# Q and K of two batches transposed by 32x32 blocks on VectorE, from blocks that DMAs set out beforehand

## The chip, the cores and the metric

The kernel runs on one core of a Trainium2 chip. A core has TensorE (matrix products and transposes into PSUM), VectorE, ScalarE, GpSimd (POOL) and SyncE (SP), each with its own queue of instructions in a fixed order, and 16 DMA engines. The metric is the device time of one execution in microseconds, the median of the runs shown. The profile is of one execution; times within it are counted from the start of its span.

## The reference

Two stages on float32 data. First a linear attention with decay, for 4 batches, 8 heads, 768 positions and a head dimension of 64; then a Fourier mixing of its output along sequence and model dimension, a normalization, and an MLP (512 to 2048 to 512) with a residual.

```
for b in range(nb):                                  # blocks of positions
    intra = einsum('bhic,bhjc->bhij', qb, kb) * Dmask
    intra = einsum('bhij,bhjd->bhid', intra, vb)
    inter = einsum('bhid,bhde->bhie', qb * lam_pow, kv_state)
    out[block] = intra + inter
    kv_state = lam_block * kv_state + einsum('bhsd,bhse->bhde', kb * rev_pow, vb)

x = out as (batch, 768, 512)
u = x + real(fft(fft(x, axis=1), axis=2))
un = (u - mean(u)) / sqrt(var(u) + 1e-6)
result = u + relu(un @ w_ch1) @ w_ch2
```

The two MLP weights come as 8-byte floating point numbers, so they are loaded as pairs of 32-bit words and decoded on the core.

## The kernel before

Attention is computed in chunks of 128 positions, six to a batch, all eight heads together. A chunk (`attn_chunk`, L257) loads k, q and v with one DMA each: rows of 64 numbers (256 B) go to `[128 positions, 8 heads, 64]`. The product of q and k contracts over the head dimension, so both must stand with the head dimension on the partitions. For this TensorE transposes pairs of heads, four 128x128 transposes for k (L272) and four for q (L277), into PSUM, and ScalarE copies the results to `kT` and `qT` (L274, L279). From these come the scores (L290, two halves of the array, one head in each), which VectorE multiplies by the decay (L294). The natural k is also multiplied by its decay on GpSimd (L268, `kd`) for the state (L305); this isn't done in the last chunk of a batch. From the second chunk on, VectorE makes `qs` from the transposed q in PSUM (L282) for the product with the state (L318). L322 multiplies scores and v, and L329 turns the output back.

The Fourier stage of a batch (`fft_ln`, L427) needs rows in mirrored order, which GpSimd gathers from a copy of x in device memory (`mirror_a`, `mirror_b`). `fold_a` and `fold_b` add and subtract rows and columns on VectorE into two pairs of tiles, `fe` and `fo`, the first with 128 rows and the second with 65 (L365 to L416). Products with tables follow on TensorE (L440, then L453 to L458), then the normalization. `mirror_a` gathers the rows that `fold_a` needs into tiles of their own, `r0` and `r1`, from the pool `fp`, which has one buffer for each name.

The weights are loaded in 32 pieces of 512 KB (`load_weights`, L219). Each goes into a `raw` buffer of the pool `hp_`, which has five buffers of this shape, and is decoded by VectorE and ScalarE together (L232 to L240). The MLP of a pair of tiles (`mlp`, L549) takes four buffers of the same pool for its hidden values (`hr`), so that the last weight loads and the first MLP group share five buffers. Four of the twelve groups go through `mlp` (L555, L569), mixed with the front stages of the batches 1 to 3; the other eight are done after them by `late` (L623), with a scheme of seven products for eight (L637, L684).

The order of work: every engine executes its instructions in program order, and that order is set before the run. The kernel is written as generators which yield an estimate of the TensorE time of each piece; `weave` (L723) interleaves two of them in a given ratio of these estimates, and at L770 and L771 the ratio for the rest of the front stages against the MLP groups is worked out from `t_rest`. A planner then orders the instructions of each engine by dependencies and its own estimates, sets the waits, and assigns buffers. So an instruction that stands early in an engine's order and has to wait holds up everything behind it on this engine, but nothing on the others that doesn't depend on it. All loads, and the stores of `ud`, `utd` and the output, are issued by SP in one order; ScalarE issues the stores of x for the gathers. In the program each DMA that SP issues also waits until the one about eight places before it in the queue has landed.

Names used below: `ld` is the pool of k, q and v (two buffers for each name), `at` the pool of the attention's intermediate tiles, `dram` a pool of tiles in device memory, `ALU.mult` elementwise multiplication.

Of the kernel before, what the change touches and what calls it, by code (L numbers as in the profile page):

```python
# [10 lines left out]
F32 = mybir.dt.float32  # L11
U32 = mybir.dt.uint32
# [63 lines left out]
def kernel(  # L76
# [10 lines left out]
    nc = tc.nc  # L87
    B, H, S, D = q.shape
    DM = H * D
    DFF = moe_w_ch1.shape[1]  # L90
    C = 128
    NC = S // C
    HC = NC // 2
    HP = H // 2
# [26 lines left out]
    ld = front_pool("ld", 2)  # L121
# [16 lines left out]
    def new(pool, shape, tag, **kw):  # L138
        cnt[0] += 1
        return pool.tile(shape, F32, tag=tag, name=f"{tag}{cnt[0]}", **kw)  # L140

    def psum_a(shape):
        return new(pa, shape, "pa")
# [58 lines left out]
    def row_of(j, n=128):  # L202
        return bass.IndirectOffsetOnAxis(ap=ix[0:n, j:j + 1], axis=0)
# [4 lines left out]
    w1v = moe_w_ch1.rearrange("(c p) f -> p c f", p=128)  # L208
    w2v = moe_w_ch2.rearrange("(c p) m -> p c m", p=128)
    WP = 512  # L210

    def load_tables(i):
        if i == 1:
# [5 lines left out]
    def load_weights(dst, src):  # L219

        if src.dtype == F32:
            nc.sync.dma_start(dst, src)
            return
        raw = hp_.tile([128, 2 * WP], U32, tag="hr", name=f"raw{cnt[0]}")
        pw = ep.tile([128, WP], U16, tag="pw", name=f"pw{cnt[0]}")
        cnt[0] += 1
        nc.sync.dma_start(raw, src.bitcast(U32))
        lo, hi = raw[:, 0:2 * WP:2], raw[:, 1:2 * WP:2]
        top = raw.bitcast(U16)[:, 3:4 * WP:4]
        lof, d = lo.bitcast(F32), dst.bitcast(U32)  # L230

        nc.vector.tensor_scalar(pw, top, 0x7FF0, None, op0=ALU.bitwise_and)  # L232
        nc.scalar.activation(pw, pw, AF.Relu, bias=cvt[:, 0:1], scale=-1.0)
        nc.scalar.activation(pw, pw, AF.Relu, bias=cvt[:, 1:2], scale=-8.0)
        nc.vector.scalar_tensor_tensor(pw, top, 0x8000, pw, op0=ALU.bitwise_and, op1=ALU.bitwise_or)  # L235

        nc.vector.tensor_scalar(d, hi, 0x000FFFFF, None, op0=ALU.bitwise_and)
        nc.scalar.activation(lof, lo, AF.Copy, scale=2.0 ** -52)
        nc.vector.scalar_tensor_tensor(dst, d, 2.0 ** -20, lof, op0=ALU.mult, op1=ALU.add)
        nc.vector.scalar_tensor_tensor(dst, dst, 1.0, pw.bitcast(BF16), op0=ALU.add, op1=ALU.mult)  # L240
# [8 lines left out]
            yield 1.0  # L249


    xs, xn_, xd = {}, {}, {}

    def pair(t, hp):
        return t[:, 2 * hp:2 * hp + 2, :].rearrange("p a d -> p (a d)")

    def attn_chunk(b, c):  # L257
        rows = slice(c * C, (c + 1) * C)
        kt, qt, vt = (new(ld, [C, H, D], nm) for nm in ("k", "q", "v"))
        for t, src in ((kt, k), (qt, q), (vt, v)):  # L260
            nc.sync.dma_start(t, src[b, :, rows, :].rearrange("h p d -> p h d"))
        if b == 0:
            load_tables(c)

        last = c == NC - 1
        if not last:
            kd = new(at, [C, H, D], "kd")
            nc.gpsimd.tensor_tensor(kd, kt, kpow, op=ALU.mult)  # L268

        ptk = psum_a([128, HP, C])  # L270
        for hp in range(HP):
            nc.tensor.transpose(ptk[:, hp, :], pair(kt, hp), ident)  # L272
        kT = new(at, [128, HP, C], "kT", bufs=2)
        nc.scalar.copy(kT, ptk)  # L274
        ptq = psum_a([128, HP, C])
        for hp in range(HP):
            nc.tensor.transpose(ptq[:, hp, :], pair(qt, hp), ident)  # L277
        qT = new(at, [128, HP, C], "qT", bufs=2)
        nc.scalar.copy(qT, ptq)  # L279
        if c > 0:  # L280
            qs = new(at, [128, HP, C], "qs")
            nc.vector.tensor_tensor(qs, ptq, qpow, op=ALU.mult)  # L282
        yield 1.2


        mm = nc.tensor.matmul
# [68 lines left out]
        nc.gpsimd.memset(t, 0.0)  # L355

    gather = nc.gpsimd.indirect_dma_start
    eo, r1s = {}, {}

    def fold_x(b, a, n, i, lo, hi):  # L360

        e, o = eo[b][a]
        tt = nc.vector.tensor_tensor

        tc.keep_in_program_order(tt(e[0:n, i, 0:DM], lo, hi, op=ALU.add))  # L365
        tc.keep_in_program_order(tt(o[0:n, i, 0:DM], lo, hi, op=ALU.subtract))
        tt(e[0:n, i, 1:HM], e[0:n, i, 1:HM], e[0:n, i, HM:DM - 1], op=ALU.add)
        tt(o[0:n, i, 1:HM], o[0:n, i, 1:HM], o[0:n, i, HM:DM - 1], op=ALU.subtract)

    def mirror_a(b):  # L370

        xa = xd[b][0]
        r1 = r1s[b] = [new(fp, [128, DM], f"r{a}") for a in range(2)]

        eo[b] = [(new(fp, [128, 2, 2 * W], f"fe{a}"), new(fp, [128, 2, 2 * W], f"fo{a}")) for a in range(2)]
        for a, n in enumerate(BLK):
            gather(out=r1[a][0:n], out_offset=None, in_=xa[:, :], in_offset=row_of(a, n))
        for t in range(2, HC):
            u = xs[b, HC + t] = new(xp, [128, DM], "x")
            gather(out=u[:, :], out_offset=None, in_=xa[:, :], in_offset=row_of(2 + t))  # L380
# [6 lines left out]
            xs[b, t] = xn_.pop((b, t))  # L387

    def fold_a(b):
        r1 = r1s.pop(b)  # L390
        for a, n in enumerate(BLK):
            fold_x(b, a, n, 1, r1[a][0:n], xn_[b, HC + a][0:n])

    def fold_b(b):

# [371 lines left out]

    run(weave(part(fr, 2 * t_chunk), weave(part(back, FO * 1.7 - 1.0), w, 0.9), 1.5))
    run(w)
    t_rest = 3 * t_front - 6 * t_chunk  # L770
    run(weave(fr, back, (len(PLAIN) * t_mlp - FO * 1.7 - 25.0) / t_rest))  # L771
    front_end.close()
    s2.wp = ctx.enter_context(tc.tile_pool(name="ws", bufs=1, side="left", reuse_waits="tile"))
# [43 lines left out]
```

## Time and profile before

| what | value |
|---|---|
| median of three runs | 882.87 us (881.8 to 887.67) |
| the profiled execution | 881.96 us, span 879.7 us |
| mean granted TensorE clock | 0.982 of full speed |
| TensorE matmul busy | 805.3 us, 92% |
| TensorE weight loads busy | 640.9 us, 73% |
| VectorE busy | 443.9 us, 50% |
| ScalarE busy | 199.1 us, 23% |
| GpSimd busy | 91.0 us, 10% |
| DMA queue of SP | 122816 packets, 57.51 MB, 25.4% of 16 engines |

The page lists each engine's busy time over the span. A TensorE matmul's end is modelled and overlaps with the next, so the distance between starts tells what one costs in a full stretch. The page divides the span into 40 slices of 22 us, with a digit of busy tenths for each engine. Groups of instructions are shown as line, engine, operation, output and inputs, shapes and count, then busy time and mean duration, then the idle time before them and what ended it. The chain of waits is followed back from the last instruction: at every step to what released it. SPq is SP's queue of DMA issues, with the time the issue itself took.

By its place in the profile, the execution has three stretches: to about 186 us the weights are loaded and decoded while batches 0 and 1 go through the attention; to about 443 us the Fourier stage of batch 1, the batches 2 and 3 and the first four MLP groups; from there to the end the eight other groups.

### The profile page before, as it was taken

What the parts mean: (1) busy time and instruction counts of PE and PEld (TensorE: products, weight loads), DVE (VectorE), ACT (ScalarE), POOL (GpSimd) and SP (SyncE); (2) the same over time, 40 slices, a digit from 0 to 9 for tenths busy, and PEclk for the clock granted to TensorE, in tenths of its full rate; (3) what the DMA queues carried; (4) which work ended last, traced back from release to release, by engine and by line L of the source; (5) the groups of instructions that cost most, each with busy time, mean ns of one, the idle gap of its engine ahead of it and who ended that gap; (6) DMA issues with size and microseconds to landing.
All of it is one profiled execution on the core that took longest, in us unless ns stands there. A gap on an engine that the chain in (4) does not pass through costs nothing.

```text
span 879.7 us, 11692 instructions
## 1 busy us (share of the span) xinstructions
PE 805.3 (92%) x4596; PEld 640.9 (73%) x4596; DVE 443.9 (50%) x1022; ACT 199.1 (23%) x451; POOL 91.0 (10%) x108
## 2 busy tenths in 40 slices
PE   4775768689999999999999999999999999999997
PEld 3564556454877557864884888888888888888886
DVE  4678969862562347425597454125611563045410
ACT  3654426630223102211210220012100220012100
POOL 2214411201021202102000000000000000000000
PEclk9989889899999999999999999999999999999999
DMA  9898426710065604643154001110111000110010
GB/s 230 228 234 253 109 84 154 229 67 26 23 142 131 166 25 115 127 87 99 37 152 105 19 1 49 48 48 1 49 48 36 13 1 9 40 48 1 1 37 24
DMA packets 128830, 72.43 MB, mean 82 GB/s; under 512 B 111200, under 2 KB 112744, under 8 KB 128776
## 3 DMA queue, kind: packets, MB, share of 16 engines
q1 hardware_dynamic: 122816, 57.51, 25.4%
q0 software_dynamic: 2496, 7.87, 2.7%
q10 hardware_dynamic: 3464, 6.30, 2.0%
q8 instruction: 36, 0.59, 0.3%
q14 instruction: 18, 0.15, 0.0%
HBM read 50.68 MB, written 20.99 MB: 81 GB/s over the span
## 4 chain that ended last, share of the span: by engine, by line
PE 71%; DVE 8%; issue 6%; DMA 4%; POOL 1%; ACT 1%; POOLq 0%; DVEq 0%; ACTq 0%
PE p L637 22%; PE p L684 22%; PE pm L555 8%; PE pm L569 8%; PE pa L440 3%; DMA raw<-in_moe_w_ch_dram 3%; PE pa L322 2%; PE pa L290 1%; DMA x<-xb,ix 1%; PE pa L318 1%; DVE pw L235 1%; PE pa L305 1%; PE pa L329 1%; PE pa L272 1%; PE pa L277 1%
## 5 line engine op out<-in xcount | busy, mean ns | idle before, releaser
L555 PE MATMUL pm<-ut,w 128*128 128x256 f32 x512 | 123.1, 389 | 10.9 <-ACT hr L563 9.2
L555 PEld LDWEIGHTS pm<-ut,w 128*128 128x128 f32 x512 | 95.0, 193 | 28.0 <-ACT hr L563 10.2
L569 PE MATMUL pm<-w,hr 128*128 128x512 f32 x256 | 114.9, 597 | 0.0
L637 PE MATMUL p<-ur,w 128*128 128x256 f32 x384 | 93.6, 380 | 0.1
L569 PEld LDWEIGHTS pm<-w,hr 128*128 128x128 f32 x256 | 47.1, 190 | 51.7 <-issue 51.1
L637 PEld LDWEIGHTS p<-ur,w 128*128 128x128 f32 x384 | 73.0, 190 | 10.6 <-issue 0.5
L637 PE MATMUL p<-us,w1s 128*128 128x256 f32 x256 | 65.2, 379 | 0.0
L684 PE MATMUL p<-w,hs 128*128 128x256 f32 x256 | 58.0, 380 | 0.5 <-DVE y L705 0.5
L684 PE MATMUL p<-w,ha 128*128 128x256 f32 x256 | 57.9, 379 | 0.0
L684 PE MATMUL p<-w2s,hs 128*128 128x256 f32 x256 | 57.9, 379 | 0.0
L545 POOL DMA_INDIRECT out_dram<-y,ix x12 | 11.8, 982 | 428.9 <-DVE y L708 368.4
L684 PEld LDWEIGHTS p<-w,hs 128*128 128x128 f32 x256 | 48.6, 190 | 7.4 <-DVE y L705 0.9
L684 PEld LDWEIGHTS p<-w,ha 128*128 128x128 f32 x256 | 48.7, 190 | 6.5
L637 PEld LDWEIGHTS p<-us,w1s 128*128 128x128 f32 x256 | 48.7, 190 | 6.5
L684 PEld LDWEIGHTS p<-w2s,hs 128*128 128x128 f32 x256 | 48.7, 190 | 6.5
L664 ACT COPY ha<-p 128x256 f32<-128x256 f32 x32 | 11.9, 372 | 172.8 <-PE p L637 172.8
L322 PE MATMUL pa<-sc,v 128*64 128x128 f32 x384 | 33.1, 298 | 11.3 <-DVE sc L294 11.3
L282 DVE TENSOR_TENSOR qs<-pa,qpow 128x512 f32<-128x512 f32 x20 | 13.8, 689 | 51.6 <-ACT qT L279 51.5
L322 PEld LDWEIGHTS pa<-sc,v 128*64 128x64 f32 x384 | 24.5, 147 | 19.4 <-DVE sc L294 14.6
L290 PE MATMUL pa<-qT,kT 64*128 64x128 f32 x384 | 29.4, 291 | 9.8 <-ACT qT L279 9.8
L290 PEld LDWEIGHTS pa<-qT,kT 64*128 64x128 f32 x384 | 24.5, 193 | 18.9 <-ACT qT L279 15.5
L675 DVE TENSOR_TENSOR ha<-p,ha 128x256 f32<-128x256 f32 x32 | 13.6, 425 | 45.6 <-ACT ha L674 45.5
(142 smaller groups left out, 1188.1 us busy)
## 6 DMA issues: line engine op xcount, KB each, us to landing
raw<-in_moe_w_ch_dram SPq DMA_DIRECT2D x32, 512.0 KB, 5.0
k<-in_k_dram SPq DMA_DIRECT2D x24, 256.0 KB, 4.4
q<-in_q_dram SPq DMA_DIRECT2D x24, 256.0 KB, 4.0
v<-in_v_dram SPq DMA_DIRECT2D x24, 256.0 KB, 3.9
ud<-x SPq DMA_DIRECT2D x16, 256.0 KB, 2.0
utd<-uq SPq DMA_DIRECT2D x64, 64.0 KB, 2.2
u<-ud SPq DMA_DIRECT2D x16, 256.0 KB, 2.6
ur<-utd SPq DMA_DIRECT2D x8, 512.0 KB, 4.4
```

The costliest lines, as they stand in the source:

```text
L235: nc.vector.scalar_tensor_tensor(pw, top, 0x8000, pw, op0=ALU.bitwise_and, op1=ALU.bitwise_or)
L282: nc.vector.tensor_tensor(qs, ptq, qpow, op=ALU.mult)
L290: mm(pss[hi][:, hp, :], lhsT=kT[HD[hi], hp, :], rhs=qT[HD[hi], hp, :], start=True, stop=True)
L322: mm(po[HD[hi], hp, :], lhsT=vt[:, 2 * hp + hi, :], rhs=sc[hi][:, hp, :], start=(c == 0 and hp == 0), stop=(hp == HP - 1), skip_group_chec ...
L440: mm = nc.tensor.matmul(ps[0:m, n, :], lhsT=piece(a, i, n), rhs=cs[0:rows, a, i in (2, 3), n, :], start=(a == 0), stop=(a == 1))
L545: nc.gpsimd.indirect_dma_start(out=out.rearrange("b s d -> (b s) d"), out_offset=row_of(2 + HC * (b + 1) + T - HC), in_=y[:, :], in_offset ...
L555: nc.tensor.matmul(ps, lhsT=w1[:, c, 128 * fc:128 * fc + 128], rhs=ut[:, c, :], start=(c == 0), stop=(c == KO - 1))
L569: nc.tensor.matmul(ps, lhsT=hr[fc // 4][:, fc % 4, 128 * i:128 * i + 128], rhs=w2[:, fc, :], start=(fc == 0), stop=(fc == FO - 1))
L637: nc.tensor.matmul(ps, lhsT=s2.A[a][:, kt, 128 * i:128 * i + 128], rhs=U[b][:, kt, :], start=(first and kt == 0), stop=(kt == 1), skip_gro ...
L664: nc.scalar.copy(a11, two(X))
L675: V.tensor_tensor(a22, two(Z), a22, op=ADD)
L684: nc.tensor.matmul(ps, lhsT=h[a][:, s, i, :], rhs=s2.B[b][:, i, :], start=(first and i == 0), stop=(i == HF - 1), skip_group_check=True)
```

## The change

For batches 2 and 3 (`TURNED`) k and q no longer go through TensorE's transposes and ScalarE's copies. Instead:

- `move_blocks` copies k and q of a batch within device memory into a tile `moved`, 16 DMAs for each of k and q, so 64 in all. One takes, for one half of the head dimension of a head and all 768 positions, pieces of 32 numbers (128 B). Four neighbouring positions stand together behind each other in the new tile. The copies of batch 2 are placed on SP behind the weight load that is ninth from the end, those of batch 3 behind the last one, by an order edge on SP alone. They are traced after the loop over the weights.
- A chunk loads its part of `moved` with one DMA each for k and q, 2 KB for each partition, and one VectorE instruction transposes all 32x32 blocks of it, with an output pattern that puts positions in order again, straight into `kT` and `qT`. So 24 VectorE transposes stand in the place of 96 TensorE transposes and 24 ScalarE copies. `qs` is computed from `qT` in SBUF and no longer from PSUM.
- The natural k is still loaded where `kd` is made (five of six chunks); the natural q isn't in these batches. The new block tile of k (`kb`) takes two buffers in `ld`; q's block tile shares the name and buffers of q.
- `r0` and `r1` are gone: the gather goes into a part of `fo`, and the fold writes its sum to `fe` and then its difference over the gathered rows.
- The first yield of a chunk of these batches is 0.3 and not 1.2, and `t_rest` is smaller by as much.

The diff, at its core:

```diff
+    def move_blocks(b, after):
+        for nm, src in (("k", k), ("q", q)):
+            m = moved[b, nm] = dram.tile([4, NC, 32, HP, 4, 32], F32, name=f"moved_{nm}{b}")
+            for a in range(4):
+                for hp in range(HP):
+                    with tc.issue_after(after):
+                        nc.sync.dma_start(m[a, :, :, hp].rearrange("c n t d -> (c n) t d"),
+                                          src[b, 2 * hp + a // 2, :, 32 * (a % 2):32 * (a % 2) + 32]
+                                          .rearrange("(n t) d -> n t d", t=4))
...
-        nc.sync.dma_start(raw, src.bitcast(U32))
+        loads.append(nc.sync.dma_start(raw, src.bitcast(U32)).ins)
...
+        def turned(nm, load, src):
+            t = new(ld, [128, HP * C], load)
+            nc.sync.dma_start(t, moved[b, src][:, c].rearrange("a n h t d -> a n (h t d)"))
+            tT = new(at, [128, HP, C], nm, bufs=2)
+            nc.vector.transpose(tT.rearrange("p h (n t) -> p h t n", t=4),
+                                t.rearrange("p (h t d) -> p h t d", h=HP, t=4))
+            return tT
+        if blocks:
+            kT, qT = turned("kT", "kb", "k"), turned("qT", "q", "q")
+            ptq = qT
+            if not last:
+                kt = natural("k", k)
+        else:
+            kt, qt = natural("k", k), natural("q", q)
+        vt = natural("v", v)
...
+        if not blocks:
             ptk = psum_a([128, HP, C])
             for hp in range(HP):
                 nc.tensor.transpose(ptk[:, hp, :], pair(kt, hp), ident)
...
-        yield 1.2
+        yield 0.3 if blocks else 1.2
...
-            gather(out=r1[a][0:n], out_offset=None, in_=xa[:, :], in_offset=row_of(a, n))
+            gather(out=eo[b][a][1][0:n, 1, 0:DM], out_offset=None, in_=xa[:, :], in_offset=row_of(a, n))
...
-            fold_x(b, a, n, 1, r1[a][0:n], xn_[b, HC + a][0:n])
+            fold_x(b, a, n, 1, eo[b][a][1][0:n, 1, 0:DM], xn_[b, HC + a][0:n])
...
     run(w)
-    t_rest = 3 * t_front - 6 * t_chunk
+    for b in TURNED:
+        move_blocks(b, loads[-9 + 8 * (b - TURNED[0])])
+    t_rest = 3 * t_front - 6 * t_chunk - 0.9 * NC * len(TURNED)
```

## The prediction

> **What bounds the kernel now.** I read the page's slices first, then the chain of waits, then each engine's timeline where the chain changes hands.
>
> ```profile
> PE   4775768689999999999999999999999999999997
> DVE  4678969862562347425597454125611563045410
> DMA  9898426710065604643154001110111000110010
> ```
>
> A slice is 22 us. From the tenth on (198 us) TensorE is at 9 tenths, so whatever TensorE loses after that point is added to the end, and its work removed there comes off. Before it, TensorE waits for the weights. The DMA row looks free from 176 to 242 us (1, 0, 0). The chain of waits from 160 to 226 us tells how the first stretch ends:
>
> ```profile
> 166.81 4.12 DMA raw<-in_moe_w_ch_dram
> ...
> 173.51 0.68 DVE pw L235
> ...
> 174.22 3.61 DMA raw<-in_moe_w_ch_dram
> ...
> 182.77 0.62 DVE pw L235
> ...
> 183.91 1.99 PE pm L555 x8
> 185.90 13.75 PE pm L569 x32
> ```
>
> A weight load lands, VectorE decodes it, the freed buffer lets the next load go or becomes the `hr` tile of the first MLP group. TensorE's L555 and L569 start when this ends. I call the last nine of the 32 loads A to I (A issued at 150.70, E at 166.81, G at 174.22, H at about 177.05, when F's decode is done, I at about 180.66, when G's is).
>
> VectorE after that (timeline, 208 to 217 us):
>
> ```profile
> 208.58 0.42 DVE L415 TENSOR_TENSOR fo<-fo 128x256 f32<-128x256 f32 x1
> 208.93 0.42 DVE L416 TENSOR_TENSOR fo<-fo 128x256 f32<-128x256 f32 x1
> 217.10 0.42 DVE L575 TENSOR_TENSOR y<-pm,x 128x256 f32<-128x256 f32 x1 [7.76 <-PE pm L569]
> ```
>
> It ends the fold of batch 1's first half, which TensorE needs for L440 at 209.62, and is idle for 7.76 us. The rows to be removed, in the full stretch (TensorE timeline, batch 3):
>
> ```profile
> 358.20 0.60 PE L329 MATMUL pa<-ident,oT 128*128 128x128 f32 x4
> 358.64 0.60 PE L272 MATMUL pa<-ident,k 128*128 128x128 f32 x4
> 359.08 0.60 PE L277 MATMUL pa<-ident,q 128*128 128x128 f32 x4
> 359.51 0.81 PE L555 MATMUL pm<-ut,w 128*128 128x256 f32 x3
> ```
>
> Starts are 0.44 us apart: that, and not the 293 ns mean of one, is what four transposes cost a full TensorE.
>
> **What the Trainium skill says.** (1) "DMA: Bandwidth & Descriptors", Queues, rings and completion order: each DMA engine consumes the descriptors of one queue in ring order. The trace agrees: loads E, G, H and I land at 170.93, 177.83, 180.60 and 184.28, in order of issue. So a copy put ahead of a weight load on SP's queue delays it. (2) Same page, Why small descriptors are slow: a fixed overhead per packet, whatever its size. It agrees: the median packet takes 13 ns at 128 B, 18 at 256 B, 84 at 2 KB and 159 at 4 KB. (3) Same page, Latency and other measured facts: copies between two places of device memory ran at 207 to 214 GB/s. The trace has no such copy; its loads peak at 410 to 416 GB/s, twice that. (4) "VectorE: DVE Perf Modes", The three transpose paths: VectorE turns 32x32 blocks only, which is why the blocks have to be moved first; the trace prices the operation (L497, 702 ns).
>
> **The change part by part.** 12 chunks (batches 2 and 3) are concerned.
>
> TensorE: 96 transposes go, 2 x 0.44 us per chunk, 12 x 0.87 = 10.4 us off the full stretch (245 to 443 us). Bounds: 8 us, if a quarter of it only widens waits that TensorE has there anyway; 14.5 us, the busy time of these rows between 245 and 443 us (6.7 + 6.6 us for the 88 records kept), scaled to 96.
>
> ScalarE: 24 copies of 0.59 us go (L274, L279), 14 us. It is 1 to 4 tenths busy there and TensorE fills the wait with L555; nothing.
>
> VectorE: 24 block transposes come, at L497's price:
>
> ```profile
> L497 DVE STREAM_TRANSPOSE uq<-un 128x512 f32<-128x512 f32 x16 | 11.2, 702 | 0.0
> ```
>
> 24 x 0.70 = 16.8 us. It is 15 to 63% busy in the 10 us windows from 250 to 410 us but one, so it is hidden; only from 340 to 350 us (10.00 of 10 busy) it can show. I take 1 us (0 to 4). `qs` reads SBUF in place of PSUM: nothing.
>
> Loads: 12 of q and 2 of k go, 24 of 256 KB in 2 KB rows come, ten more. A packet of 84 ns, 8 per engine, is 0.67 us each, while the DMA engines are about half idle: nothing. The `r` tiles fold into `fo`: the gather of batch 2 starts at 296.47, the last L440 reading the old `fo` was issued before 230; nothing. The planner's smaller yields leave TensorE's order nearly as it was.
>
> The copies: 64 DMAs of 192 x 4 pieces of 128 B, 768 packets, 48 per DMA engine, 98 KB. Nothing in the trace goes from device memory to device memory in 128 B pieces. Lower bound: 48 x 13 ns = 0.62 us, the price of packets of that size. Upper: if reading and writing device memory cost twice a load's price, as (3) has it, 48 x 2 x 13 ns = 1.25 us, and 1.95 us at 20 ns, a little above the 18 ns of the 256 B loads, since half of the pieces start in the middle of a 256 B row. Nearest row:
>
> ```profile
> 246.95 2.66 SPq L501 DMA_DIRECT2D utd<-uq  x4
> ```
>
> Four writes of 512 such packets each in 2.6 us, 0.65 us each; by packets 768/512 x 0.65 = 0.98 us. I take s = 0.98 us per copy, all in, whether SP's issue or the engines limit it.
>
> Where they stand: in the changed program's order SP has A, 1 copy, B, 3, C, 2, D, 8, E, F, 8, G, 1, H, 5, I, then 36 copies, then the store of the first y, then the block loads of chunk 0. Two things follow.
>
> *First, the weight tail.* I walk the queue: a weight load occupies the engines 8 x 159 ns = 1.28 us, starts about 1.4 us after its issue or when what is ahead is done, and E, G, H keep their own waits for buffers. B ends at 156.2; two stores of x (8 x 84 ns each) and 3 copies: C starts at 160.5 and not 158.4. After 2 copies D at 163.7 (161.2 before). After 8 copies and three gathers (2.1 us, 8 packets of 84 ns per engine each) E at 174.9 (168.2): 6.7 late. E, F, 8 copies: G at 185.3 (175.6): 9.7 late. H at 187.6 (178.45): 9.1 late. L555 at 183.91, L569 and all behind it move by **9 us**. Bounds: 2 us at s = 0.62, 30 at 1.95.
>
> *Second, a new wait.* I starts at 193.8; with 1.3 us for itself and 36 x 0.98 = 35.3 us for the copies, the block load of chunk 0 (0.7 us, and 1 us to be seen) is in at 232 us. In the changed program's order VectorE's first block transpose stands inside the fold of batch 1, just before the two operations that are L415 and L416 above. VectorE gets there at 208.6 + 9 = 217.7 and waits **14 us**. Behind it in its queue stand these two, for which TensorE's L440 waits, the three other transposes, `qs`, the y additions (for which POOL's gather at 218.12 and SP's stores wait), the second half of the fold and the relus. TensorE has two L569 matmuls left and then stops, so nothing covers it. Bounds: 0 us at s = 0.62 (ready at 210), 54 at 1.95. The other three transposes (2.1 us) and `qs` then fall into the old 7.76 us gap: nothing. The gather beside the copies is late too, but still ahead of the same wait.
>
> Sum: 9 + 14 + 1 - 10.4 = 13.6 us on the profiled execution's 881.96 (span 879.7): 895. The median shown is 882.87, 0.9 us above it, which is left out as spread.
>
> **Rivals.** *The copies are cheap* (s = 0.62 to 0.7): engines at the floor of 13 ns. For it: the four `utd` writes come in bursts of 135 to 148 GB/s, so 0.65 us is SP's issue and not the engines. Tail 2 to 3, wait 0 to 3, transposes 1, less 10.4: 874 to 878, faster. It decides below s = 0.78, where tail and wait together equal the saving. Against it: all 768 packets read and write the same memory, and half of the reads start in the middle of a 256 B row.
>
> *The copies cost double* (s = 1.3 to 1.95): tail 16 to 30, wait 27 to 54: 916 to 957. For it: (3). Against it: that figure is for large rows, which are bound by bytes, and these are bound by packets.
>
> *The wait is there, but the saving isn't*: TensorE finds other waits (decode, relus behind transposes on VectorE), as at 340 to 350 us where VectorE is full: 10 us above the first case, 905.
>
> **How the numbers follow.** About 1% (9 us) is what a measurement tells from no change. Middle case (s from 0.8 to 1.3): 0.52, 883 to 916, likeliest 895. Cheap copies: 0.24. Double: 0.16. Saving lost: 0.08. Cheap copies give faster than 873 in under half of their cases: 0.11 faster. Within 1% are the rest of these and the middle case up to s = 0.9 (891): 0.29. Slower: 0.60. The range leaves out the fastest tenth (under 876) and the slowest (over 930, s about 1.5).
>
> **What would show it.** The copies' time from issue to landing, and their spacing on SP after the last weight load: 0.98 us each, 35 us for 36. L569's first start at 195 and not 185.9. VectorE idle before its first block transpose, put down to the DMA of the blocks, about 14 us, and TensorE idle before L440's second half as long. Four-transpose groups of k and q absent in batches 2 and 3, and the attention chunks 0.87 us closer. The prediction is wrong if the spacing is under 0.8 us (then no wait, and a gain), or if TensorE has other work in front of the fold.

## The result, and the profile after

| | before | after |
|---|---|---|
| median of the runs compared | 884.8 us (881.8 to 887.67, 4 runs) | 919.0 us (916.41 to 921.76, 4 runs) |
| ratio, 95% interval | | 1.0388 [1.0347, 1.0429] |
| the profiled execution | 881.96 us, span 879.7 us | 917.21 us, span 915.4 us |
| mean granted TensorE clock | 0.982 | 0.960 |

The change makes the kernel 3.9% slower, some 34 us, where 13.6 were forecast. The page's slices of the changed kernel (22.9 us each) show where to look:

```profile
PE   4765687677899877999999999999999999999997
DVE  4789869653358343774659455215531364125410
PEclk9998789788789988999999999999999999999999
DMA  9998417986205551254225300200011100110000
```

TensorE is no longer at 9 tenths from the tenth slice on: the 10th and 11th read 7 and 8, the 15th and 16th 7 and 7. In the same four slices the clock row reads 8, 7, 8, 8. The DMA row, which was 1, 0, 0 before in the 9th to 11th slices, now reads 8, 6, 2.

To add the loss up, I cut both executions at the same work: I, to the last weight decode on VectorE; II, to the first bn_stats (the VectorE instruction that opens the normalization of a tile) of batch 1 (the seventh in the trace; my expectations, which count from zero, call it the sixth); III, to the first bn_stats of batch 2, so with the hand-over from batch 2 to 3; IV, to the last bn_stats; V, the rest. The view of windows gives each stretch: length, TensorE busy with its number of matmuls, then its weight loads, VectorE, ScalarE and GpSimd, then granted clock, DMA share and GB/s. Before, II and III:

```profile
186.40:232.90 46.50, 44.79 (x157) 26.75 (x156) 18.80 (x44) 5.47 (x15) 2.90 (x3) 1.00 0.07 23
232.90:335.60 102.70, 99.78 (x712) 71.31 (x711) 47.19 (x109) 22.33 (x57) 16.45 (x21) 1.00 0.42 99
```

After, II and III:

```profile
194.40:259.70 65.30, 55.38 (x157) 33.70 (x156) 23.82 (x50) 5.24 (x15) 2.91 (x3) 0.83 0.47 102
259.70:375.10 115.40, 100.87 (x665) 70.02 (x664) 60.77 (x121) 16.14 (x45) 17.75 (x21) 0.94 0.37 100
```

In II the same 157 matmuls keep TensorE busy for 55.38 us in place of 44.79, at a clock of 0.83; and it is idle for 65.30 - 55.38 = 9.9 us in place of 1.7. In III 47 matmuls fewer take 1.1 us more, at 0.94, and idle time grows from 2.9 to 14.5 us. The whole:

| stretch | before us | after us | difference |
|---|---|---|---|
| I | 186.4 | 194.4 | +8.0 |
| II | 46.5 | 65.3 | +18.8: idle +8.2, clock +10.6 |
| III | 102.7 | 115.4 | +12.7: idle +11.6, busy +1.1 |
| IV | 112.3 | 106.6 | -5.7 |
| V | 431.8 | 433.7 | +1.9 |
| sum | 879.7 | 915.4 | +35.7 |

As a gain the saving shows only in IV: 58 matmuls fewer, 6.1 us less busy. V has eight matmuls more, moved there.

**The tail of the weights.** The chain of waits has the first MLP group (L591 and L605 are L555 and L569 of before) 8.1 us later, 193.96 against 185.90:

```profile
190.18 3.78 PE pm L591 x8
193.96 14.91 PE pm L605 x32
```

**SP's queue, then.** Its timeline (start, time of the issue, what):

```profile
190.82 12.27 SPq L265 DMA_DIRECT2D moved_k<-in_k_dram  x16
203.13 12.25 SPq L265 DMA_DIRECT2D moved_q<-in_q_dram  x16
215.79 0.35 SPq L579 DMA_DIRECT2D out_dram<-y  x1
216.19 0.62 SPq L286 DMA_DIRECT2D kb<-moved_k  x1
...
219.09 2.78 SPq L280 DMA_DIRECT2D v<-in_v_dram  x1
221.92 5.46 SPq L280 DMA_DIRECT2D k<-in_k_dram  x1
```

A copy takes 12.26 / 16 = 0.77 us. What stands at 190.82 are batch **3**'s copies, for work that starts after 320 us. Behind them stand batch **2**'s first loads, needed at 219 us: block loads and natural k and v alike. Before, k, q and v of this batch were loaded between 151 and 164 us.

The block loads are also slow in themselves. The first, issued at 216.19, is used at 222.84, 6.65 us later, and not because the DMA engines are full. In these two windows block loads are nearly all that moves (the last two numbers are the engines' busy share and GB/s):

```profile
220.00:223.00 3.00, 0.76 (x2) 0.00 (x0) 0.16 (x1) 0.00 (x0) 0.00 (x0) 1.00 0.30 105
336.00:339.00 3.00, 3.00 (x9) 1.33 (x8) 0.76 (x2) 0.00 (x0) 1.00 (x1) 1.00 0.26 99
```

By the packets' times in the trace, some 85 ns each, about four are in flight at once. In e1 (below), whose loads read 2 KB rows of k and q in place, there are up to about 16, and the share from 286 to 287 us is 0.83. The source of a block load has four parts as its outermost dimension (`a` in `a n h t d`); that this makes the difference is likely, and no run changed it alone.

**VectorE and TensorE at the first fold.** VectorE's timeline, with the idle time before an instruction and what ended it in brackets:

```profile
218.24 0.42 DVE L449 TENSOR_TENSOR fo<-fo 128x255 f32<-128x255 f32 x1
222.84 1.08 DVE L288 STREAM_TRANSPOSE kT<-kb 128x512 f32<-128x512 f32 x1 [4.17 <-DMA kb<-moved_k]
223.77 0.41 DVE L451 TENSOR_TENSOR fo<-fo 128x256 f32<-128x256 f32 x1
...
241.89 0.69 DVE L403 TENSOR_TENSOR fe<-x,x 65x512 f32<-65x512 f32 x1 [4.13 <-DMA x<-xb,ix]
```

TensorE's, with the products of batch 1's fold (L476, before L440):

```profile
224.32 1.62 PE L476 MATMUL pa<-cs,fo 128*128 128x193 f32 x4 [3.57 <-DVE fo L451]
...
244.25 6.25 PE L476 MATMUL pa<-cs,fe 65*1 65x193 f32 x18 [3.94 <-DVE fe L441]
```

The block transpose waits where the prediction put it, ahead of L451, for 4.17 us; TensorE stops for 3.57 us behind it. There is a second stop that the prediction doesn't have: the gather of the other 65 rows, issued at 234.90, is seen after 7.0 us, and TensorE stops again for 3.94. After the stops the records show half the clock for 6.8 us from 223.5 and for 13.7 us from 244.0: half of 20.5 us is 10.2. With 1.8 us at the beginning of II, which belong to an earlier stretch of half clock (189.3 to 196.2), it is 11.1, close to the 10.6 us of II's table. The Trainium skill, "TensorE: Matmul & The Clock Gate", Part 1: The HAM clock gate, has the rule: after an idle window of about 3.4 us TensorE falls to half its clock and needs at least one busy window of that length to come back. For the fall the traces of this study agree. I took all stops of over 2 us between 200 and 700 us in the 16 traces other than e3's, counted from the end of one TensorE weight load to the start of the next (up to 0.9 us more than the brackets show, which count between matmuls; stops given below without a bracket are counted in this way too). Of 28 stops of 2.1 to 3.2 us 27 left the clock alone, a stop of 3.6 us did too, and of 32 stops of 3.7 us or more 31 were followed by half clock; the remaining one began while the clock was halved already. For the way back a single window doesn't always do: most stretches end 3 to 6 us after the matmuls go on, but the one after the second stop lasts 13.7 us, here and in e5, e6 and e7, with no stop in it.

**The hand-over from batch 2 to 3** (TensorE's timeline; L328 scores, L360 scores times v):

```profile
316.29 1.09 PE L356 MATMUL pa<-qs,st 64*64 64x128 f32 x16
324.79 0.69 PE L360 MATMUL pa<-sc,v 128*64 128x128 f32 x2 [7.42 <-DVE sc L332]
...
347.86 1.63 PE L476 MATMUL pa<-cs,fe 128*128 128x193 f32 x4 [4.97 <-DVE fe L445]
```

and the chain of waits that ends at 324.79:

```profile
315.58 6.86 DMA fo<-xa,ix
...
322.54 0.69 DVE fe L403
323.23 0.99 DVE kT L288
324.22 0.53 DVE sc L332
...
324.79 0.69 PE pa L360 x2
```

The multiplication of the last chunk's scores (L332) is ready to run, but on VectorE the first fold operation (L403) and a block transpose of batch 3 stand ahead of it, and L403 waits for a gather that takes 6.86 us. Before, the scores (L294) came first, and the fold (L365) after them:

```profile
296.24 1.29 DVE L294 TENSOR_TENSOR sc<-pa,decay 128x512 f32<-128x512 f32 x2 [1.70 <-PE pa L290]
299.94 0.69 DVE L365 TENSOR_TENSOR fe<-r,xn 128x512 f32<-128x512 f32 x1 [2.41 <-DMA r<-xa,ix]
```

### The profile page after: what moved, and what is told of

Same layout as the page of the kernel before. It is cut to its first block, busy times and chain, and to the rows that moved or that the text cites. A ratio compares the mean times of both kernels' runs of the same rounds, so it can differ in the third digit from the quotient of the medians.

```text
span 915.4 us, 11553 instructions
## 1 busy us (share of the span) xinstructions
PE 812.5 (89%) x4500; PEld 639.9 (70%) x4500; DVE 471.1 (51%) x1046; ACT 186.7 (20%) x427; POOL 87.3 (10%) x108
## 4 chain that ended last, share of the span: by engine, by line
PE 69%; DVE 10%; DMA 8%; issue 7%; ACT 2%; POOL 1%; POOLq 0%; SPq 0%; DVEq 0%; ACTq 0%
PE p L673 21%; PE p L720 21%; PE pm L591 8%; PE pm L605 7%; DMA raw<-in_moe_w_ch_dram 4%; PE pa L476 3%; PE pa L360 2%; DMA fo<-xa,ix 2%; PE pa L328 2%; DMA x<-xb,ix 1%; PE pa L356 1%; DVE pw L236 1%; PE pa L367 1%; PE pa L343 1%; DVE w L240 1%
## 5 line engine op out<-in xcount | busy, mean ns | idle before, releaser
L591 PE MATMUL pm<-ut,w 128*128 128x256 f32 x512 | 126.6, 396 | 16.9 <-ACT hr L599 15.0
L591 PEld LDWEIGHTS pm<-ut,w 128*128 128x128 f32 x512 | 96.5, 196 | 35.8 <-ACT hr L599 16.9
L605 PE MATMUL pm<-w,hr 128*128 128x512 f32 x256 | 118.7, 616 | 0.0
L605 PEld LDWEIGHTS pm<-w,hr 128*128 128x128 f32 x256 | 49.3, 197 | 56.9 <-issue 56.6
L581 POOL DMA_INDIRECT out_dram<-y,ix x12 | 11.8, 984 | 430.8 <-DVE y L744 368.4
L360 PE MATMUL pa<-sc,v 128*64 128x128 f32 x384 | 33.6, 292 | 20.5 <-DVE sc L332 20.5
L360 PEld LDWEIGHTS pa<-sc,v 128*64 128x64 f32 x384 | 24.4, 143 | 30.4 <-DVE sc L332 24.9
L328 PE MATMUL pa<-qT,kT 64*128 64x128 f32 x384 | 30.4, 291 | 10.9 <-ACT qT L317 9.6
L332 DVE TENSOR_TENSOR sc<-pa,decay 128x512 f32<-128x512 f32 x48 | 31.3, 678 | 15.8 <-PE pa L328 13.0
L328 PEld LDWEIGHTS pa<-qT,kT 64*128 64x128 f32 x384 | 25.3, 193 | 18.8 <-ACT qT L317 12.3
L711 DVE TENSOR_TENSOR ha<-p,ha 128x256 f32<-128x256 f32 x32 | 13.6, 425 | 45.6 <-ACT ha L710 45.5
```

Source lines behind the costliest of these rows:

```text
L328: mm(pss[hi][:, hp, :], lhsT=kT[HD[hi], hp, :], rhs=qT[HD[hi], hp, :], start=True, stop=True)
L332: nc.vector.tensor_tensor(t, pss[hi], decay[:, hi::2, :], op=ALU.mult)
L360: mm(po[HD[hi], hp, :], lhsT=vt[:, 2 * hp + hi, :], rhs=sc[hi][:, hp, :], start=(c == 0 and hp == 0), stop=(hp == HP - 1), skip_group_chec ...
L581: nc.gpsimd.indirect_dma_start(out=out.rearrange("b s d -> (b s) d"), out_offset=row_of(2 + HC * (b + 1) + T - HC), in_=y[:, :], in_offset ...
L591: nc.tensor.matmul(ps, lhsT=w1[:, c, 128 * fc:128 * fc + 128], rhs=ut[:, c, :], start=(c == 0), stop=(c == KO - 1))
L605: nc.tensor.matmul(ps, lhsT=hr[fc // 4][:, fc % 4, 128 * i:128 * i + 128], rhs=w2[:, fc, :], start=(fc == 0), stop=(fc == FO - 1))
```

## The experiments

Two theories at the start. A: the copies make the loss. B: the turning itself, with its order on VectorE, does. "Tail" is how much more time than before passes from the 24th weight decode to the 32nd; it doesn't depend on where the execution began, which varies by some 8 us in the profiles of these kernels. Lengths of II, III and IV are of the profiled executions. Each ratio is against runs of the kernel before that were made with it, with medians from 882.58 to 884.8 us.

| run | median us | ratio [95%] | tail | II | III | IV |
|---|---|---|---|---|---|---|
| before | 884.8 | | 0 | 46.5 | 102.7 | 112.3 |
| after | 919.0 | 1.0388 [1.0347, 1.0429] | +8.1 | 65.3 | 115.4 | 106.6 |
| e1 no copies | 889.26 | 1.006 [1.0038, 1.0082] | +4.2 | 45.3 | 108.6 | 106.5 |
| e2 copies only | 895.02 | 1.011 [1.0055, 1.0164] | +7.0 | 48.0 | 103.0 | 112.4 |
| e3 pause | 883.91 | 0.9983 [0.9966, 1.0] | +0.2 | 46.6 | 103.0 | 112.3 |
| e4 direct loads | 931.46 | 1.0529 [1.0481, 1.0577] | +7.0 | 46.3 | 119.1 | 141.2 |
| e5 turn after fold | 907.54 | 1.0268 [1.0214, 1.0322] | +8.2 | 58.1 | 109.7 | 108.4 |
| e6 fold after scores | 915.41 | 1.0383 [1.035, 1.0416] | +6.4 | 64.3 | 112.6 | 107.2 |
| e7 both orders | 905.08 | 1.0247 [1.0224, 1.027] | +8.0 | 58.2 | 106.5 | 107.6 |
| e8 copies after weights | 922.85 | 1.0466 [1.0444, 1.0488] | -0.6 | 78.0 | 113.3 | 106.5 |
| e9 batch 3's copies later | 911.7 | 1.0326 [1.0292, 1.0361] | +7.4 | 53.2 | 121.2 | 104.5 |
| e10 e9 and both orders | 902.51 | 1.0215 [1.0183, 1.0247] | +8.8 | 47.6 | 121.5 | 104.6 |
| e11 batch 3 only, ordered | 892.13 | 1.0081 [1.0053, 1.0109] | +0.8 | 46.7 | 114.2 | 104.5 |
| e12 no copies, ordered | 884.17 | 1.0005 [0.9988, 1.0023] | +4.7 | 45.3 | 104.5 | 106.6 |
| e13 batch 2 only, ordered | 892.6 | 1.0097 [1.0059, 1.0135] | +10.0 | 47.1 | 100.3 | 111.2 |
| e14 the same, GpSimd's queue | 889.12 | 1.0055 [1.0035, 1.0076] | +4.4 | 48.0 | 104.3 | 110.8 |
| e15 e12, pace of before | 885.47 | 1.0019 [1.0001, 1.0038] | +4.1 | 45.9 | 102.6 | 99.1 |

**e1**: no copies, and the block loads read 2 KB rows of k and q in place.

```diff
-    for b in TURNED:
-        move_blocks(b, loads[-9 + 8 * (b - TURNED[0])])
...
-            nc.sync.dma_start(t, moved[b, src][:, c].rearrange("a n h t d -> a n (h t d)"))
+            nc.sync.dma_start(t, rows2k[rows])
```

> The 64 copies are left out; the block loads read 2 KB rows of k and q in place, so the block transposes work on numbers in the wrong order (the scores are not the reference's), at the same loads and the same VectorE work. Theory A (the copies make the whole loss: the weight tail and the wait of the first block transpose): tail and wait are gone, the 96 TensorE transposes stay gone: 872 to 878 us. Theory B (VectorE's queue: block transposes and the early fold wait for DMAs in the second half of the stretch, and each stop of TensorE is followed by a time at half clock): the 12 us lost between the first and the second Fourier stage stay: 884 to 892 us.

II is whole again (45.3 us). The run takes away two things, the copies and the slow block loads. The copies' part is shown by e7 and e10 below: both have slow loads and the same order on VectorE, and II is 58.2 us with batch 3's copies in their old place and 47.6 with them elsewhere. But the run isn't faster than before: III is still 5.9 us longer, and the tail 4 us late. Some of the loss belongs to the turning. For the tail the likely reason stands on VectorE: without copies to wait for, four block transposes, at 172.44, 173.37, 181.40 and 183.00 us, 4.4 us in all, come among the last weight decodes (in e12 and e15 too).

**e2**: the kernel before, with the 64 copies at the same places, unread.

```diff
     run(w)
+    for b in TURNED:
+        move_blocks(b, loads[-9 + 8 * (b - TURNED[0])])
```

> The kernel before with the 64 copies added at the same places of SP's queue, read by nobody; TensorE's transposes stay, VectorE has nothing new. Both theories: the weight tail is 8 us late. Theory A (loss by what the copies occupy): also the gathers beside them are late, 893 to 897 us. Theory B: without a transpose that waits on VectorE TensorE doesn't stop at the fold, so no half clock beyond a short one: 891 to 895 us. Over 905 us would mean that the copies alone, by contention, make most of the loss, and the waiting transposes little.

The copies alone cost about 10 us of median, most of it in the tail. II is 1.5 us longer; so copies in the queue don't stop TensorE by themselves. It takes loads and transposes that wait behind them.

**e3**: the kernel before, with one fold addition repeated 12 times on VectorE where the block transpose would wait.

```diff
             tt(bm[:, 1, 1:HM], lo, hi, op=ALU.add)
+            if b == 1 and a == 0:
+                for _ in range(12):
+                    tt(bm[:, 1, 1:HM], lo, hi, op=ALU.add)
```

> The kernel before with one addition of the fold of batch 1 (0.335 us from start to start) repeated 12 times more, same input and output, 4.0 us on VectorE just where the first block transpose stands in the changed kernel. If a stop of TensorE costs only its own length: 885 to 887 us, and the granted clock stays at 1.00 from 186 us on. If a stop of this length is followed by half clock, as the trace of the changed kernel shows at 223 and 244 us: one stretch of 6.8 us at 0.5 and 888 to 892 us.

No cost, and no test of the stop either: the planner, who knows of these operations, set 14 second-layer matmuls ahead of the products, and TensorE didn't stop. It covered a delay that it knew of; one that it doesn't know of wasn't tried in this way.

**e4**: block tiles loaded straight from k and q, four DMAs of 128 pieces of 896 B each in the place of one, no copies.

```diff
-            nc.sync.dma_start(t, moved[b, src][:, c].rearrange("a n h t d -> a n (h t d)"))
+            for a in range(4):
+                run_ = s[b, a // 2::2, rows, :].rearrange("h (n t) d -> n h (t d)", t=4)
+                nc.sync.dma_start(t[32 * a:32 * a + 32], run_[:, :, 32 * (a % 2):32 * (a % 2) + 224])
...
-            kT, qT = turned("kT", "kb", "k"), turned("qT", "q", "q")
+            kT, qT = turned("kT", "q", "k"), turned("qT", "q", "q")
```

> No copies in device memory: the block tile is loaded straight from k and q by four DMAs, each of 128 pieces of 896 B (56 numbers beyond need between the blocks), and the transposes read its blocks at a step of 64. Theory A: the gain of TensorE shows, 872 to 878 us. Theory B: the tail and the first wait are gone, but block loads of SP's queue still come late in the second half: 880 to 892 us.

Slower than with copies. 29 us of its loss stand in IV, where a store of `y` waits 23.3 us in SP's queue ahead of other stores; from 492 us on TensorE stops for 14.7 and 19.3 us, the second time in V. Block tiles of k share the two buffers of q's here, so the run doesn't price direct loads alone. I didn't follow it further: it doesn't replace the copies.

**e5, e6, e7**: the order on VectorE, by order edges: the block transposes of a batch behind the last fold operation of the batch ahead; the first half of a fold behind the last chunk's scores; both.

```diff
+            with tc.issue_after(folded[b - 1]):
+                nc.vector.transpose(...)
...
+            with tc.issue_after(scored[b]):
+                fold_x(b, a, n, 1, eo[b][a][1][0:n, 1, 0:DM], xn_[b, HC + a][0:n])
```

> The changed kernel with one edge more on VectorE: each block transpose of a batch is issued after the last fold instruction of the batch ahead of it. Copies, loads and everything else stay. Theory A (what costs 17 us between the first y and the sixth bn_stats is VectorE's order: the block transposes stand ahead of the folds, wait for moved blocks, and the folds with the TensorE products behind them wait too): that stretch goes back to within 4 us of the kernel before, no TensorE stop over 2.5 us there, clock at 1.0; total 900 to 906. Theory B (the copies keep the DMA engines and the queue so busy that gathers and stores of the fold come late by themselves): the stop stays, 914 to 921.

> The changed kernel with the first half of each batch's fold issued on VectorE after the last chunk's score multiplications. Theory A (the 7.4 us stop of TensorE at 317 comes from the fold that waits for its gather ahead of the scores): that stop is under 3 us, total 907 to 913. Theory B (the last chunk's block load, late behind stores in SP's queue, sets that time by itself): the stop stays 5 us or more, total 916 to 921.

> Both orders together. If both A theories hold, the effects add: 888 to 897, the tail of the weight loads (+8 to 9 us) being all that is left over the kernel before, less some of the TensorE transposes saved. If the waits only move to other places: 908 or more.

e5 and e7 do part of what was expected, and by its total e6 can't be told from the change (1.0383 against 1.0388); what each order does is seen in the traces. In e5 the first stop of II is gone (7.6 us between the first and second `y` become 0.5), with its half clock; but the second stop stays (4.2 us, then 13.7 us of half clock), and II is 58.1 us. It comes from the late gather and not from the order. In e6 the stop ahead of L360 falls from 7.7 to 4.3 us, but the next one grows from 5.8 to 8.2. Both together give back 12 to 14 us of 34 (by ratios, or by medians); III of e7 is 8.9 us shorter than that of the change.

**e8**: all copies behind the last weight load.

```diff
-        move_blocks(b, loads[-9 + 8 * (b - TURNED[0])])
+        move_blocks(b, loads[-1])
```

> The changed kernel with all 64 copies behind the last weight load. Theory A (the tail is late because 32 copies stand between weight loads in SP's queue): the last weight decode is within 3 us of the kernel before, in place of 8 late; but the first block load now comes some 25 us later (32 copies of 0.77 us), so VectorE waits for the moved blocks some 12 to 25 us and the stop of TensorE at the first fold grows: total 920 to 940. Theory B (the tail is late for other reasons, as it was 3 to 4 us late with no copies at all): the decode stays 6 us or more late.

A on both counts: the tail is back to that of before (-0.6), and II grows to 78.0 us, with stops of 11.8 and 9.1 us and 37.5 us of half clock in one piece. So the 8 us of the tail do come from the copies' place among the weight loads.

**e9, e10**: batch 3's copies no longer behind the last weight load but behind the loads of batch 2's chunks 2 to 4; e10 with both orders.

```diff
+        if b == 2:
+            for a in {2: (0, 1), 3: (2,), 4: (3,)}.get(c, ()):
+                move_blocks(3, behind[0], a)
...
-    for b in TURNED:
-        move_blocks(b, loads[-9 + 8 * (b - TURNED[0])])
+    move_blocks(2, loads[-9])
```

> The changed kernel with batch 3's 32 copies taken from behind the last weight load and put, 16, 8 and 8, behind the loads of batch 2's chunks 2, 3 and 4; batch 2's copies stay, and VectorE's order is left to the planner. Theory A (these 32 copies, 24.5 us of SP's queue, stand ahead of batch 2's own first loads, which then come at 216 us, make VectorE wait, and share the DMA engines with the two gathers of the fold): the stretch from the first y to the sixth bn_stats is within 3 us of the kernel before, clock at 1.0 there, the tail of the weight loads 6 to 8 us late as in the changed kernel; total 899 to 906. Theory B (the moved blocks are late because batch 2's own copies take so long): VectorE still waits 4 us or more and the total is 912 or more.

> The same with both orders on VectorE (block transposes after the fold of the batch ahead, first half of the fold after the last chunk's scores). If copies' place and the fold's place are two separate causes, it takes both away and keeps the tail only: 888 to 897. If the copies, now among batch 2's stores and loads, hold back the chunks there: 903 or more.

In e9 the second stop of II is gone, in e10 both: II is 47.6 us, at a clock of 0.98. So II's loss takes two things: batch 3's copies ahead of batch 2's loads, and block transposes ahead of the fold on VectorE. But the totals missed. III grew to 121 us, since the copies now delay the stores and loads of batch 2: in e10 eight copies, from 312.96 to 321.66, stand ahead of a block load of q for which TensorE stops at 328 us. I found no free place for them in SP's queue.

**e11**: only batch 3 turned, ordered, its copies as in e9.

```diff
-    TURNED = range(2, B)
+    TURNED = range(3, B)
```

> Only batch 3 turned by blocks, its copies behind the loads of batch 2's chunks 2 to 4, nothing behind the weight loads, fold after scores. If the copies cost nothing where SP's queue and the DMA engines have room, the saved TensorE transposes of one batch are left, some 4 us as in the run without copies: 877 to 882 and faster than the kernel before. If 0.77 us of queue per copy holds back loads and stores there as well: 888 or more.

Slower than before by 0.8%: IV gives 7.8 us, III takes 11.5. The copies from 261 to 305 us sit in one queue with batch 2's loads; the gathers at the hand-over come late and TensorE stops for 4.1 and 3.9 us.

**e12**: e1 with the fold behind the scores (the edge of e6).

> The run without copies (block loads read rows of k and q in place, so the scores of the last two batches are not the reference's), now with the first half of the fold after the last chunk's scores. Theory A (its loss between the last stage of batch 1 and the fold of batch 2, 8 us, is the stop of TensorE behind the early fold): 880 to 884, the saved transposes showing. Theory B (the stop has another cause, as a late block load behind stores): 887 to 890, unchanged.

This is the turning without copies, without slow block loads and without the bad order: no difference from before. 5 us better than e1, as A says, and not a gain. III is still 1.8 us longer than before, with a stop of 5.8 us at 310, and the tail 4.7 us late.

**e13, e14**: batch 2 alone turned, ordered, its 32 copies in SP's queue as in the change, or (e14) in GpSimd's, which is empty there. In both the block loads come behind the last weight load.

```diff
-    TURNED = range(2, B)
+    TURNED = range(2, 3)
...
-                        nc.sync.dma_start(m[a, :, :, hp].rearrange(...), ...)
+                        nc.gpsimd.dma_start(m[a, :, :, hp].rearrange(...), ...)
```

> Only batch 2 turned by blocks, its 32 copies among the weight loads in SP's queue as in the changed kernel, batch 3 left as in the kernel before, both orders on VectorE kept. Theory A (batch 2's copies cost the tail of the weight loads, 8 us, and nothing later; batch 3's copies make all the rest of the early loss): last weight decode 6 to 9 us late against the decode before the copies, no loss from the first y to the sixth bn_stats, total 888 to 894. Theory B (a batch turned by blocks has a loss of its own later, whoever's copies): 896 or more.

> The same with the 32 copies issued from GpSimd's queue, behind its gathers of batch 1, so that no copy stands ahead of a weight load in SP's queue, while the copies still share the DMA engines with them. Theory A (the tail is lost in SP's queue): the last weight decode is 0 to 3 us late, total 5 to 8 us under the run with SP's queue. Theory B (the tail is lost on the DMA engines, which move 12288 packets of 128 bytes beside the weights): decode 6 us late or more, total equal within 3 us or higher.

e13 is theory A: the tail (+10), and nothing lost later, though its block loads are as slow as those of the change. It also prices the saving where nothing stops. TensorE's timeline at the same place as shown for the change (L363 is L360 there), and the window of III:

```profile
303.22 0.43 PE L363 MATMUL pa<-sc,v 128*64 128x128 f32 x2
...
320.92 0.90 PE L480 MATMUL pa<-cs,fe 128*128 128x193 f32 x4 [1.50 <-DVE fe L449]
```

```profile
245.50:345.80 100.30, 96.18 (x664) 67.26 (x663) 55.38 (x117) 16.14 (x45) 17.20 (x21) 1.00 0.41 103
```

The stops of 7.42 and 4.97 us are 0 and 1.50, the clock is 1.00, and 48 matmuls fewer than before take 99.78 - 96.18 = 3.6 us less. III of the change has as many matmuls (665) and takes 100.87: 4.7 us are the clock's. In e14 GpSimd issues 16 copies in 13.84 and 14.06 us, 0.87 us each, from 163.0 to 190.9, beside the same weight loads. The tail is 4.4 us late, between what theories A and B had said, so 5.6 us less than in e13; the medians differ by 3.5 us, with intervals that overlap. But the queue isn't all that changed. DMA queues (packets, MB, share of 16 engines) of e13, then of e14:

```profile
q1 hardware_dynamic: 142208, 61.97, 27.3%
q0 software_dynamic: 2496, 7.87, 2.8%
```

```profile
q1 hardware_dynamic: 117120, 58.82, 25.2%
q0 software_dynamic: 4032, 11.02, 4.2%
```

SP's queue (q1) loses the 24576 packets of 128 B that 32 copies make (the expectation says 12288). GpSimd's (q0) gains only 1536, for the same 3.1 MB: 1024 packets of 2 and 4 KB, and 512 of 4 B. So the 5.6 us go with the copies' place in SP's queue or with their small packets, and the run doesn't part the two. The 4.4 us that are left most likely come from the copies on the shared DMA engines. VectorE waits longer for two of the last weight loads of e14, issued at 166.38 and 182.79:

```profile
172.02 0.78 DVE L233 TENSOR_SCALAR pw<-raw 128x512 uint16<-128x512 uint16 x1 [2.91 <-DMA raw<-in_moe_w_ch_dram]
188.28 0.43 DVE L233 TENSOR_SCALAR pw<-raw 128x512 uint16<-128x512 uint16 x1 [1.34 <-DMA raw<-in_moe_w_ch_dram]
```

That is 5.6 and 5.5 us from issue to use, where the same loads took 4.2 and 3.7 before; in e8, with no copy beside the weights, the last one took 3.8 and the tail wasn't late. The tail of e1 and e12, also 4 us late, has another likely reason, as said: no block transpose stands among the decodes of e14.

**e15**: e12 with `t_rest` as before.

```diff
-    t_rest = 3 * t_front - 6 * t_chunk - 0.9 * NC * len(TURNED)
+    t_rest = 3 * t_front - 6 * t_chunk
```

> The ordered run without copies, with one term of the change undone: the pace at which feed-forward work is woven between the attention chunks is worked out as in the kernel before (nothing taken off for the turned batches). The scores of the last two batches are not the reference's. Theory A (the saved transposes are given back at the hand-over from batch 2 to 3 because the quicker pace uses up the feed-forward products that cover the round trip of the last chunk, stop of 5.8 us at 310): the stop falls under 3 us and the total to 878 to 881. Theory B (the round trip is bare whatever the pace): 883 to 885, unchanged.

B. The stop at the hand-over is 4.3 us in place of 5.8 and IV is 7.5 us shorter, but those matmuls are then done in V: no gain. No version tried is faster than the kernel before.

## Why the prediction was wrong

By its sum, 9 + 14 + 1 - 10.4 = 13.6, against 35.7 in the trace:

- **Tail, 9**: right, 8.0, in part by luck. A copy took 0.77 us and not 0.98, and the prediction itself says that at 0.78 tail and wait together just equal the saving: with the measured price its sum would have come to about no change. e8 and e13 confirm that copies among the weight loads make the tail; e14 leaves 4.4 us of it with the copies out of SP's queue, which is likely the engines that they share with the weights.
- **New wait at the first block transpose, 14, and VectorE, 1**: the place and the mechanism were right, the terms weren't. II lost 18.8: 8.2 of idle TensorE and 10.6 of half clock, for which the sum has no term. The wait itself was 4.17 us: the copies were quicker. On the other side the block load took 6.6 us from its issue to the transpose and not 1.7, since its packets went four at a time and not over all 16 engines ("8 per engine"), and it was not the only load held back. "The gather beside the copies is late too, but still ahead of the same wait" holds for the gather of the 128 rows (4.3 us, 3.4 before). The sum has nothing for the next one, of the 65 rows: it comes after that wait, takes 7.0 us beside block loads where it took 3.2, and makes the costlier of the two stops. That 15 comes near 18.8 is luck. e5 against e7 and e10 shows the two apart.
- **TensorE, -10.4**: this is the step that failed. "96 transposes go ... off the full stretch" takes for granted that TensorE stays full and at full clock. III, IV and V together gave +12.7 - 5.7 + 1.9 = +8.9. That is 19.3 of the 22.1 us that the sum missed; II accounts for 3.8 and the tail for -1.0. The saving exists: 3.6 us in III (e13), 6.1 in IV, less 1.9 of moved work, 7.8 in all. What ate it is 11.6 us of idle in III, at the hand-over from batch 2 to 3, and 4.7 of half clock there. The forecast walked VectorE's queue once, at batch 1's fold, and not at batch 2's, where two things of the same kind meet: fold operations that wait for a gather ahead of the scores (e6, e12), and gathers slowed by the next batch's block loads (in e7 VectorE waits 7.68 us for the xb gather there, in e13, where the next batch isn't turned, 4.10).
- **Twenty-four block transposes at 0.70 us**: 1.1 us each. In the change VectorE's load isn't seen to cost anything by itself; what costs is where the transposes stand in its order.
- **Rivals**: "the wait is there, but the saving isn't" was the right one, with a chance of 0.08 and a price of 10 us, where 19 was lost; the places that it names for it (decode, relus, 340 to 350 us) were not the ones. "The cheap copies" had the copy's price about right (0.77, under its 0.78) and the sign wrong: "under 0.8 (then no wait, and a gain)" fails: at 0.77 there was a wait of 4.17 us, and a loss. The copy's price didn't decide; what waits behind the copies did.

The range (876 to 930) held 919.0 and the chance of slower was the largest.

Open: why a stop of 5.8 us (e12) to 7.0 us (e7) remains at the hand-over with the fold behind the scores when batch 3 is turned, and not when it isn't (e13). A gather slowed by block loads fits e7; in e12 block transposes stand among the fold's operations. Neither was taken away alone. Nor was a block load tried that spreads over all engines, with the copies kept. The half clock was seen to follow the stops, and its cost was read from windows with equal numbers of matmuls; keeping TensorE busy through a stop wasn't tried.

## What to carry to other kernels

In this kernel a stop of TensorE over about 3.5 us cost its length plus half of the 3 to 14 us, mostly 7, that followed at half clock. Price a load by how many of its packets are in flight at once, and not by its bytes alone: a new layout can change it. When DMAs are added to a queue, list everything that comes behind them, loads of other batches too, and ask of each when it is needed: here copies for work 130 us later stood ahead of loads needed at once. A saving on a full engine counts only if the next hand-over (store, gather, fold) doesn't turn it into a wait; walk every such place, and not the first alone.

## What the runs showed of the hardware

- A copy from device memory to device memory of 768 pieces of 128 B: 0.77 us each, issued in a row by SP. Its packets took 13 ns in the median, as such packets did in the kernel before and not twice that; 48 of them are 0.62 us of an engine, and from 191 to 215 us the 16 engines were 0.85 busy. Issued by GpSimd (e14) the same copies took 0.87 us each and went in packets of 2 and 4 KB.
- A load of 256 KB in 2 KB rows whose source has four parts outermost kept about four packets in flight, and the 16 engines 0.26 to 0.30 busy; one with 128 rows outermost (e1) up to 16.
- The block transpose of 128x512 takes 1.1 us where its output pattern puts positions in order again, 0.70 us with plain patterns.
- A gather of rows was seen after 3.2 to 3.4 us with quiet DMA engines, after 4.3 us beside the copies, and after 6.8 to 7.0 us beside block loads.
- Half clock lasted 6.8 us most often, else 3.4, 10.2 or 13.7, once 20.5 (e4) and once 37.5 (e8): multiples of 3.4.
